# A sigmoid attention and bilinear FFN kernel: weight decoding in six VectorE operations on larger pieces, casts moved to ScalarE, no GpSimd work in the first twelve pairs of heads

## The chip, the core and the metric

The kernel runs on one core of one Trainium2 chip. The metric is the device time of one execution in microseconds (us). Engine names are those of the profile: PE is TensorE (PEld its weight loads), DVE is VectorE, ACT is ScalarE, POOL is GpSimd, SP is SyncE, which here only issues DMAs.

## What is computed

```python
# q, k, v: 8 batches x 12 heads x 448 positions x 64; weights are handed over as float64
scores = q @ k.T / sqrt(64) - log(448)
attn   = 1 / (1 + exp(-scores))            # a sigmoid, no softmax
x      = (attn @ v), heads side by side    # [3584, 768]
h      = (x @ w1) * (x @ w2)               # [3584, 1024]
out    = (h @ w3) @ w_out                  # [3584, 768]
```

## The kernel before

**Precision.** Most products run in float32r passes. An operand x is split into a hi part (a cast to float32r) and a lo part (x minus hi), and a product is hi·hi + hi·lo + lo·hi. So every operand costs a cast and a subtraction somewhere. `split` (L63) is that pair of instructions, with the engine of each given by the caller.

**Weights.** They arrive as float64 words, read as pairs of uint32. `load_words` (L67) brings a piece, `magnitude` (L72) takes the absolute value of the high words on ACT into a tile `f`, and `decode` (L77) makes float32 out of it with seven operations on DVE (L81 to L99; the last, an addition, on POOL for w3). Then `split` makes the hi and lo weights: the cast on DVE, the subtraction on POOL. `decode_weights` (L263) is a generator: one `next` of it (a *take*) issues the loads ahead, the magnitudes ahead, one decode and one split. A piece of w1 or w2 is 128 rows by 384 columns, 32 pieces in all, two for each operand of the product with a chunk of features; w3 follows in 24 pieces that go back to memory.

**Attention and the first product.** The work runs over 48 pairs of heads, six for each batch. A pair has four *slots*, one for each chunk of keys (the short one of 64 keys comes second). Slots are counted from 0, so that pair p begins at slot 4p and batch 1 at slot 24. In a slot PE computes the scores of the chunk (L183), ACT the sigmoid (L168, tile `ap` in plain pairs), and PE multiplies the attention of the slot before by v (L232 in plain pairs, L239 in the others). Two PSUM buffers hold scores. The first twelve pairs are *plain*: attention and v stay in float32 there, and DVE and POOL are left to the weights. From the third slot of batch 1 on (slot 26), PE also computes the product of the batch before with w1 and w2 (L302, tile `up`), twelve matmuls in each slot; a chunk of features takes 36 of them, three slots, and its product `g` (L313) goes to memory.

**Preparation of a pair.** `split_pair` (L136) makes qs, kh and kl of the next pair. It is issued in the second slot of a pair (for pair 1, in the first slot of pair 0). In plain pairs before the change: the cast of q and its lo part on DVE (L141, L142), the cast of k on ACT, kl on POOL; for pairs 0 and 1 all of it on DVE. The loads of q and k share three buffers, so that a load waits until the split two tiles back is done.

**Order.** PE and SP keep to the order in which the code is written, from beginning to end. ACT and POOL do so too for pairs 0 and 1 only (`if p == 2` closes that); after that, and on DVE throughout, a planner orders the instructions. A take that is written in a slot of pairs 0 or 1 thus puts its magnitudes, and any cast of it that is on ACT, ahead of the sigmoid of the next slot.

**Deal of the pieces.** `pieces` says how many takes each slot of batch 0 has (nine in all, the first in slot 3); in batch 1 every slot has one; later batches have four each.

**Afterwards.** While the last batch's product with w1 and w2 runs, w_out is decoded; then w3 w_out (L441) and the final product (L459) follow.

Of the kernel before, what the change touches and what calls it, by code (L numbers as in the profile page):

```python
# [11 lines left out]
F32 = mybir.dt.float32  # L12
# [6 lines left out]
# high words of 2**-127 and 2**128 as float64, read as the float32 of their bits  # L19
HW_MIN, HW_MAX = (float(np.uint32(e << 20).view(np.float32)) for e in (896, 1151))  # L20
# [3 lines left out]
def sigmoid_attention_bilinear_ffn(  # L24
    ctx: ExitStack,
    tc: tile.TileContext,
    qT: bass.AP,     # [B, D, H, S]
    kT: bass.AP,     # [B, D, H, S]
    v: bass.AP,      # [B, S, H*D]
    w1: bass.AP,     # [DM, 2*DF], float64 words as uint32 pairs, as all weights  # L30
    w2: bass.AP,     # [DM, 2*DF]
    w3T: bass.AP,    # [DF (columns of w3), 2*DF (rows of w3)]
    w_out: bass.AP,  # [DF, 2*DM]
    out: bass.AP,    # [B*S, DM]
):
# [100 lines left out]
    def split_pair(plain, first, qq, kk):  # L136
        """q as (hi; lo) in the rows; hi and lo of k, each twice in the rows."""
        qs = pa.tile([P, 2, S], F32R, name="qs")
        kh = pa.tile([P, 2, S], F32R, name="kh")
        kl = pa.tile([P, 2, S], F32R, name="kl")  # L140
        nc.vector.tensor_copy(out=qs, in_=qq)  # L141
        nc.vector.tensor_tensor(out=qs[D:], in0=qq[D:], in1=qs[D:], op=ALU.subtract)  # L142
        if first:
            split(kh, kl, kk, nc.vector.tensor_copy, nc.vector)
        else:
            split(kh, kl, kk, nc.scalar.copy if plain else nc.vector.tensor_copy, nc.gpsimd)
        if plain:
            return qs, kh, kl, None
        # the short chunk of head 0 as (hi, lo), of head 1 as (lo, hi)
        ks = pa.tile([P, 2, P], F32R, name="ks")  # L150
        for j in range(2):
            for i, k in ((j, kh), (1 - j, kl)):
                nc.gpsimd.tensor_copy(out=ks[:, j, i * D:(i + 1) * D], in_=k[:, j, S - D:])
        return qs, kh, kl, ks

    def split_v(plain, vv):
        if plain:
            return vv
        # head 0 as (hi, lo), head 1 as (lo, hi)
        vs = pa.tile([P, NC, 2, 2, D], F32R, name="vs")  # L160
# [9 lines left out]
    def add_halves(dst, src):  # L170
        """Both halves of src[0] to the first half of dst, of src[1] to the second."""
# [14 lines left out]
    def attention(plain, sp):  # L186
        """Attention from its scores, as operands for attend."""
# [12 lines left out]
        al = pa.tile([P, 2, S], F32R, name="al")  # L200
# [3 lines left out]
    def short_scores(ks, qs):  # L204
        """Scores of both heads for the short chunk of keys, head by head in the rows."""
        # kh q and kl q apart, in one pass per head
# [3 lines left out]
        t = pa.tile([P, S], F32, name="st", bufs=1)  # L210
# [3 lines left out]
    def short_attention(t):  # L214
        # hi and lo share the rows of one pass
# [28 lines left out]
    def combine(b, accs):  # L244
# [5 lines left out]
        t = pm.tile([P, S], F32, name="t")  # L250
# [12 lines left out]
    def decode_weights():  # L263
        """w1 and w2 as operands, then w3 as float32 back to memory; a piece at a time."""
        step = NK // 2
        jobs = [
            (n, fc, slice(at, at + step), words(w, slice(fc * P, (fc + 1) * P)))
            for fc in range(NF) for n, w in ((1, w1), (2, w2)) for at in range(0, NK, step)
# [6 lines left out]
        # while attention leaves its buffers of hi and lo idle, they serve here  # L275
        buffers = ((pd, "raw"), (pa, "vs"), (pa, "al"))
        raws, fs = [], []
        for i, (n, at, cs, _) in enumerate(jobs):
            while len(raws) <= min(i + (3 if i < n_up else 1), len(jobs) - 1):
                k = len(raws)  # L280
                _, _, ks, src = jobs[k]
                raws.append(load_words(src[:, ks], *buffers[k // 2 % 3 if k < n_up - 6 else 0]))
            while len(fs) <= min(i + 1, len(jobs) - 1):
# [10 lines left out]
    def up(b, xs, banks):  # L294
        """g = (x w1) * (x w2) of batch b, feature chunk by feature chunk; yields at each matmul."""
# [52 lines left out]
    # a slot per chunk of keys: its scores, products with the first weights, and the slot before's  # L348
    # attention times v; the short chunk of keys second, as it takes longest
    chunks = [0, NC - 1, *range(1, NC - 1)]  # L350
    ups = -(-(NF * 2 * NK * 3) // (NPAIR * NC))
    # pieces of weights per slot of the first batch
    pieces = ((0, 0, 0, 1), (0, 1, 0, 1), (0, 1, 0, 0), (0, 1, 0, 1), (0, 1, 0, 0), (0, 1, 0, 1))
    slot = 0
    for p, (b, hp) in enumerate(pairs):
# [52 lines left out]
    for jc in range(NF):  # L408
        take(filler, 10)
        for half in range(2):  # L410
# [3 lines left out]
            f = decode(raw, magnitude(raw), nc.vector)  # L414
# [77 lines left out]
```

## Time and profile before

| | |
|---|---|
| median of 3 runs | 1121.01 us (1120.77 to 1122.05) |
| span of the profiled execution | 1121.6 us; no time apart from the span is given for it |
| busy: PE, DVE, ACT, POOL | 1084.7, 777.7, 544.4, 295.1 us |
| granted TensorE clock, mean | 0.991 of full |
| DMA traffic | 133.26 MB, 119 GB/s over the span |

The profile is one execution. The busy time of an engine is a sum over the whole span, and the stages of this kernel have different limits: what bounds one of them is read from the idle time of PE in that stage and from what ended it. An instruction whose record is longer than that of others of its kind was held up while it ran.

### The profile page before, as it was taken

To read this page: it belongs to the slowest core of one execution; us is meant where nothing else is said; L and a number is where in the kernel's file an instruction comes from. 1 tells how busy PE (TensorE), PEld (TensorE's weight loads), DVE (VectorE), ACT (ScalarE), POOL (GpSimd) and SP (SyncE) were. 2 spreads that over 40 slices of the span, in tenths; PEclk is the share of its full clock that TensorE was granted. 3 is DMA by queue.
4 is the path that set the end of the run, shared out by engine and by line. 5 is a ranking of instruction groups with operands and counts; after the bars stand their busy time and mean duration, and the time that the engine had idled before them with its cause. 6 is when DMAs were issued, how large, how long until landed. Compare 5 with 4: busy or idle time off the path is not lost.

```text
span 1121.6 us, 15243 instructions
## 1 busy us (share of the span) xinstructions
PE 1084.7 (97%) x5424; PEld 964.5 (86%) x5424; DVE 777.7 (69%) x1281; ACT 544.4 (49%) x780; POOL 295.1 (26%) x322
## 2 busy tenths in 40 slices
PE   6889888999999999999999999999999999999998
PEld 2346656899999999999999998899999999999998
DVE  6999999988888888888888888958932222223222
ACT  4653333677676776767767676673322111111110
POOL 1535435433434344343343434400000000000000
PEclk9889999999999999999999999999999999999999
DMA  9576444553543535435354355305441033333331
GB/s 239 142 196 167 136 110 120 150 136 101 149 109 94 141 101 149 103 97 143 101 149 106 92 145 143 100 27 164 124 130 38 16 123 100 116 114 106 117 106 50
DMA packets 116043, 133.26 MB, mean 119 GB/s; under 512 B 9216, under 2 KB 100608, under 8 KB 115968
## 3 DMA queue, kind: packets, MB, share of 16 engines
q1 hardware_dynamic: 115968, 132.29, 42.5%
q8 instruction: 43, 0.70, 0.3%
q14 instruction: 32, 0.26, 0.1%
HBM read 102.37 MB, written 29.88 MB: 118 GB/s over the span
## 4 chain that ended last, share of the span: by engine, by line
PE 75%; DVE 11%; issue 6%; DMA 4%; POOL 2%; SPq 1%; ACT 1%; DVEq 0%; POOLq 0%; ACTq 0%
PE up L302 31%; PE up L459 21%; PE av L239 8%; PE sp L183 7%; PE up L441 6%; POOL kl L65 1%; DMA raw<-w 1%; DVE raw L96 1%; DVE f L86 1%; PE sp L209 1%; DVE qs L142 1%; DVE f L93 1%; DVE f L99 1%; DVE raw L81 1%; DMA vv<-vL 1%
## 5 line engine op out<-in xcount | busy, mean ns | idle before, releaser
L302 PE MATMUL up<-xh,w 128*128 128x448 f32 x1536 | 467.4, 368 | 2.2 <-ACT a_sb L310 2.2
L302 PEld LDWEIGHTS up<-xh,w 128*128 128x128 f32 x1536 | 289.2, 188 | 29.3 <-ACT a_sb L310 2.6
L302 PE MATMUL up<-xl,w 128*128 128x448 f32 x768 | 281.8, 367 | 0.0
L459 PE MATMUL up<-w,gh 128*128 128x384 f32 x896 | 227.5, 334 | 0.0
L65 POOL TENSOR_TENSOR kl<-kk,kh 128x896 fp32r<-128x896 f32 x46 | 128.7, 2798 | 144.8 <-DVE kh L64 68.2
L459 PEld LDWEIGHTS up<-w,gh 128*128 128x128 f32 x896 | 161.9, 188 | 0.0
L302 PEld LDWEIGHTS up<-xl,w 128*128 128x128 f32 x768 | 144.5, 188 | 13.1
L459 PE MATMUL up<-w,gl 128*128 128x384 f32 x448 | 149.6, 334 | 0.0
L168 ACT ACTIVATE ah<-sp,bias 128x896 fp32r<-128x896 f32 x108 | 108.6, 1006 | 77.3 <-PE sp L183 77.0
L463 DVE COPY o_sb<-up 128x384 f32<-128x384 f32 x56 | 31.2, 558 | 160.2 <-PE up L459 160.2
L201 DVE TENSOR_TENSOR al<-sp,ah 128x896 fp32r<-128x896 f32 x108 | 117.5, 1088 | 23.3 <-ACT sp L168 21.6
L183 PE MATMUL sp<-qs,kh 128*128 128x448 f32 (+1 forms) x312 | 122.0, 391 | 9.1 <-DVE kh L64 8.0
L183 PE MATMUL sp<-qs,kl 128*128 128x448 f32 (+1 forms) x312 | 117.9, 378 | 5.9 <-POOL kl L65 5.5
L64 ACT CAST gh<-graw 128x1024 fp32r<-128x1024 f32 x28 | 29.5, 1053 | 192.0 <-PE up L459 189.3
L65 POOL TENSOR_TENSOR vs<-vv,vs 128x256 fp32r<-128x256 f32 x72 | 58.5, 827 | 188.4 <-DVE vs L64 140.8
L168 ACT ACTIVATE sp<-sp,bias 128x896 f32<-128x896 f32 x108 | 105.1, 973 | 0.0
L183 PEld LDWEIGHTS sp<-qs,kh 128*128 128x128 f32 (+1 forms) x312 | 58.9, 189 | 50.5 <-issue 37.2
L239 PE MATMUL av<-ah,vs 128*128 128x448 f32 x288 | 94.9, 370 | 3.0 <-DVE t L175 2.0
L74 ACT ACTIVATE f<-raw 128x384 f32<-128x384 f32 (+1 forms) x72 | 38.5, 541 | 97.4 <-POOL w L65 39.1
L459 PEld LDWEIGHTS up<-w,gl 128*128 128x128 f32 x448 | 84.1, 188 | 0.0
L239 PE MATMUL av<-al,vs 128*128 128x448 f32 x216 | 80.0, 370 | 4.2 <-DVE al L201 3.9
L65 POOL TENSOR_TENSOR w<-f,w 128x384 fp32r<-128x384 f32 x32 | 48.9, 1532 | 97.0 <-DVE w L64 95.0
(58 smaller groups left out, 1479.6 us busy)
## 6 DMA issues: line engine op xcount, KB each, us to landing
qq<-qT SPq DMA_DIRECT2D x96, 224.0 KB, 3.8
kk<-kT SPq DMA_DIRECT2D x96, 224.0 KB, 3.9
g_dram<-g SPq DMA_DIRECT2D x64, 224.0 KB, 2.0
graw<-g_dram SPq DMA_DIRECT2D x28, 512.0 KB, 3.7
raw<-w SPq DMA_DIRECT2D x32, 384.0 KB, 4.6
out<-o_sb SPq DMA_DIRECT2D x56, 192.0 KB, 1.9
vv<-vL SPq DMA_DIRECT2D x48, 192.0 KB, 3.8
raw<-w3T SPq DMA_DIRECT2D x16, 384.0 KB, 4.1
```

The lines of the kernel that those rows point to most:

```text
L64: hi_engine(out=dst_hi, in_=src)
L65: lo_engine.tensor_tensor(out=dst_lo, in0=src, in1=dst_hi, op=ALU.subtract)
L74: nc.scalar.activation(f, raw[..., 1].bitcast(F32), AF.Abs)
L81: nc.vector.tensor_scalar(out=high, in0=high, scalar1=0x80000000, scalar2=0x40000000, op0=ALU.bitwise_and, op1=ALU.bitwise_xor,)
L168: nc.scalar.activation(dst, src, AF.Sigmoid, bias=bias[:n], scale=scale)
L183: nc.tensor.matmul(sp[:, j], k[:, j, at:at + n], qs[:, j], start=m == 0, stop=m == 1)
L201: nc.vector.tensor_tensor(out=al, in0=sp, in1=ah, op=ALU.subtract)
L239: nc.tensor.matmul(accs[j][:, :S], v[:, c, j].rearrange("p u d -> p (u d)"), a[:, j], start=first and m == 0, stop=last and m == len(ops) - 1,
L302: nc.tensor.matmul(acc[:, :S], w[:, fc, kc], x, start=(kc == 0 and m == 0), stop=(kc == NK - 1 and m == 2),)
L441: nc.tensor.matmul(acc[:, :NM], a[:, jc], w[:, jc, ms], start=(jc == 0 and m == 0), stop=(jc == NF - 1 and m == 2),)
L459: nc.tensor.matmul(acc[:, :NM], a[:, fc], w[:, fc, ms], start=(fc == 0 and m == 0), stop=(fc == NF - 1 and m == 2),)
L463: nc.vector.tensor_copy(out=o_sb[:, ms], in_=acc[:, :NM])
```

## The change

- `decode` has six operations instead of seven. The scale 2^-16 that the magnitude now applies moves the exponent so that a left shift by 3 does what a left shift by 4 and a right shift by 1 did, and shift and exclusive-or become one `scalar_tensor_tensor`. The last addition is on DVE always.
- A piece of w1 or w2 has 768 columns a partition instead of 384: 16 pieces instead of 32, one for each operand and chunk of features. Their raw words have a pool of their own with three buffers (`pp`), closed at pair 11; tiles that only the other pairs need (ks, vs, al, st) then come from a pool `pf` opened in its place. The tile `f` has two buffers instead of three, `t` one instead of two. A piece of w3 has 384 columns as before, or 256.
- The hi cast of a piece of w1 or w2 moves from DVE to ACT, its lo subtraction from POOL to DVE.
- In plain pairs the cast of q moves from DVE to ACT (not for pairs 0 and 1), kl moves from POOL to DVE (it was there for pairs 0 and 1); for pairs 0 and 1 the cast of k moves from DVE to ACT.
- The takes: slots 1, 7, 13 and 19 in batch 0, two slots in three of batch 1 (slots 24, 25, 27, 28, ... 46), later batches as before.

```diff
     def magnitude(raw):
-        f = pd.tile([P, *raw.shape[1:-1]], F32, name="f", bufs=3)
-        nc.scalar.activation(f, raw[..., 1].bitcast(F32), AF.Abs)
+        f = pd.tile([P, *raw.shape[1:-1]], F32, name="f")
+        nc.scalar.activation(f, raw[..., 1].bitcast(F32), AF.Abs, scale=HW_SCALE)
...
         nc.vector.tensor_scalar(out=f, in0=f, scalar1=HW_MIN, scalar2=HW_MAX, op0=ALU.max, op1=ALU.min)
-        nc.vector.tensor_scalar(
-            out=fb, in0=fb, scalar1=4, scalar2=1,
-            op0=ALU.logical_shift_left, op1=ALU.logical_shift_right,
+        nc.vector.scalar_tensor_tensor(
+            out=fb, in0=fb, scalar=3, in1=high, op0=ALU.logical_shift_left, op1=ALU.bitwise_xor
         )
-        nc.vector.tensor_tensor(out=fb, in0=fb, in1=high, op=ALU.bitwise_xor)
...
-        add_engine.tensor_tensor(out=f, in0=f, in1=r, op=ALU.add)
+        nc.vector.tensor_tensor(out=f, in0=f, in1=r, op=ALU.add)
...
-        nc.vector.tensor_copy(out=qs, in_=qq)
+        copy = nc.scalar.copy if plain else nc.vector.tensor_copy
+        (nc.vector.tensor_copy if first else copy)(out=qs, in_=qq)
         nc.vector.tensor_tensor(out=qs[D:], in0=qq[D:], in1=qs[D:], op=ALU.subtract)
-        if first:
-            split(kh, kl, kk, nc.vector.tensor_copy, nc.vector)
-        else:
-            split(kh, kl, kk, nc.scalar.copy if plain else nc.vector.tensor_copy, nc.gpsimd)
+        split(kh, kl, kk, copy, nc.vector if plain else nc.gpsimd)
...
         for i, (n, at, cs, _) in enumerate(jobs):
+            end = n_up if i < n_up else len(jobs)
+            while len(raws) < min(i + (3 if i < n_up else 2), end):
+                _, _, ks, src = jobs[len(raws)]
+                raws.append(load_words(src[:, ks], pp if len(raws) < n_up else pd))
+            while len(fs) < min(i + 2, end):
+                fs.append(magnitude(raws[len(fs)]))
+            f = decode(raws[i], fs[i])
             if n == 3:
-                f = decode(raws[i], fs[i], nc.gpsimd)
                 nc.sync.dma_start(out=w3_dram[at, :, cs], in_=f)
             else:
-                f = decode(raws[i], fs[i], nc.vector)
-                split(wh[n][:, at, cs], wl[n][:, at, cs], f, nc.vector.tensor_copy, nc.gpsimd)
+                split(wh[n][:, at, cs], wl[n][:, at, cs], f, nc.scalar.copy, nc.vector)
...
-    pieces = ((0, 0, 0, 1), (0, 1, 0, 1), (0, 1, 0, 0), (0, 1, 0, 1), (0, 1, 0, 0), (0, 1, 0, 1))
+    pieces = {1, 7, 13, 19} | {NPAIR * NC + i for i in range(3 * NF) if i % 3 < 2}
...
+        if p == PLAIN - 1:
+            take(weights, 2 * NF - len(pieces & set(range(slot))))
+            phase_p.close()
+            pf.append(phase_a.enter_context(tc.tile_pool(name="pf", bufs=2, side="right")))
...
-            if b == 0:
-                take(weights, pieces[hp % len(pieces)][i])
-            elif b == 1 or hp % 3 < 2 and i == 1:
+            if slot in pieces or b > 1 and hp % 3 < 2 and i == 1:
                 take(weights, 1)
```

## Rows read from the trace of the kernel before

**Rows 1.** The page: DVE's busy share in 40 slices of 28 us, in tenths.

```profile
DVE  6999999988888888888888888958932222223222
```

**Rows 2.** Stretches of the span: busy time of each engine, granted clock, DMA share, GB/s.

```profile
core 0: us, PE busy (x) PEld busy (x) DVE busy (x) ACT busy (x) POOL busy (x), PEclk, DMA share, GB/s
10.40:72.80 62.40, 52.77 (x194) 21.90 (x192) 55.28 (x94) 35.84 (x45) 27.22 (x14) 0.89 0.72 183
72.80:185.70 112.90, 104.47 (x471) 72.29 (x469) 109.22 (x209) 44.47 (x66) 48.49 (x33) 0.98 0.56 155
185.70:224.50 38.80, 33.98 (x155) 29.75 (x154) 35.93 (x59) 23.05 (x34) 18.47 (x24) 0.96 0.44 120
224.50:754.40 529.90, 527.52 (x2571) 481.48 (x2570) 437.76 (x689) 375.04 (x543) 200.72 (x247) 1.00 0.44 116
```

**Rows 3.** PE's timeline: start us, us; score matmuls of slots 2, 3, 8, 10, 45, 46.

```profile
15.52 0.47 PE L183 MATMUL sp<-qs,kh 128*128 128x448 f32 x1
...
17.43 0.47 PE L183 MATMUL sp<-qs,kh 128*128 128x448 f32 x1
...
32.09 0.74 PE L183 MATMUL sp<-qs,kl 128*128 128x448 f32 x1 [5.47 <-POOL kl L65]
...
37.95 0.47 PE L183 MATMUL sp<-qs,kh 128*128 128x448 f32 x1
...
172.56 0.47 PE L183 MATMUL sp<-qs,kh 128*128 128x448 f32 x1
...
176.94 0.47 PE L183 MATMUL sp<-qs,kh 128*128 128x448 f32 x1
```

**Rows 4.** Groups of instructions, 0 to 186 us, DVE and POOL: busy, mean ns.

```profile
L99 DVE TENSOR_TENSOR f<-f,raw 128x384 f32<-128x384 f32 x32 | 22.9, 716 | 0.3
L142 DVE TENSOR_TENSOR qs<-qq,qs 64x896 fp32r<-64x896 f32 x14 | 20.7, 1476 | 0.5
...
L95 DVE TENSOR_SCALAR raw<-f 128x384 uint32<-128x384 uint32 x32 | 13.9, 436 | 0.2
...
L65 POOL TENSOR_TENSOR w<-f,w 128x384 fp32r<-128x384 f32 x32 | 48.9, 1532 | 97.0 <-DVE w L64 95.0 <-PE sp L183 2.0
```

**Rows 5.** Timeline of DVE beside POOL: operations alone and beside a GpSimd subtraction.

```profile
7.97 1.09 DVE L65 TENSOR_TENSOR kl<-kk,kh 128x896 fp32r<-128x896 f32 x1
...
9.09 0.63 DVE L141 CAST qs<-qq 128x896 fp32r<-128x896 f32 x1
...
88.33 2.24 POOL L65 TENSOR_TENSOR kl<-kk,kh 128x896 fp32r<-128x896 f32 x1
...
88.50 2.29 DVE L86 TENSOR_SCALAR f<-f 128x384 f32<-128x384 f32 x1
...
92.64 0.35 DVE L86 TENSOR_SCALAR f<-f 128x384 f32<-128x384 f32 x1
...
94.11 0.55 DVE L93 TENSOR_TENSOR f<-f,raw 128x384 uint32<-128x384 uint32 x1
```

**Rows 6.** Timeline, 14 to 24 us, of ACT and DVE: sigmoids, casts, first pieces.

```profile
14.73 1.01 ACT L168 ACTIVATE ap<-sp,bias 128x896 f32<-128x896 f32 x1 [1.59 <-PE sp L183]
...
18.79 0.56 ACT L74 ACTIVATE f<-raw 128x384 f32<-128x384 f32 x1 [1.08 <-DMA raw<-w]
...
19.38 0.36 DVE L81 TENSOR_SCALAR raw<-raw 128x384 uint32<-128x384 uint32 x1 [1.00 <-ACT f L74]
...
19.92 0.55 ACT L74 ACTIVATE f<-raw 128x384 f32<-128x384 f32 x1 [0.57 <-DMA raw<-w]
...
22.58 0.94 ACT L64 CAST kh<-kk 128x896 fp32r<-128x896 f32 x1
...
23.46 0.35 DVE L64 CAST w<-f 128x384 fp32r<-128x384 f32 x1
```

**Rows 7.** Groups of instructions of ACT, whole span: busy, mean ns.

```profile
L74 ACT ACTIVATE f<-raw 128x384 f32<-128x384 f32 x64 | 35.0, 554 | 94.0 <-POOL w L65 39.1 <-DMA raw<-w_out 24.5 <-DMA raw<-w 21.2
L64 ACT CAST woh<-f 128x384 fp32r<-128x384 f32 x16 | 8.0, 511 | 10.2 <-DVE f L99 7.3 <-PE up L302 2.8
```

More of the change, by code (lines that the diff above doesn't have):

```diff
@@ L17 @@
 PSUM = bass.MemoryType.PSUM
-HW_MIN, HW_MAX = (float(np.uint32(e << 20).view(np.float32)) for e in (896, 1151))
+HW_SCALE = 2.0 ** -16
+HW_MIN, HW_MAX = (float(np.uint32((e - 128) << 20).view(np.float32)) for e in (896, 1151))
 @with_exitstack
@@ L65, in split, with load_words @@
         lo_engine.tensor_tensor(out=dst_lo, in0=src, in1=dst_hi, op=ALU.subtract)
-    def load_words(src, pool=pd, tag="raw"):
-        raw = pool.tile([P, *src.shape[1:-1], 2], U32, name="raw", tag=tag, bufs=2)
+    def load_words(src, pool=pd):
+        raw = pool.tile([P, *src.shape[1:-1], 2], U32, name="raw")
         nc.sync.dma_start(out=raw, in_=src)
@@ L72, in magnitude, with decode @@
     def magnitude(raw):
-        f = pd.tile([P, *raw.shape[1:-1]], F32, name="f", bufs=3)
-        nc.scalar.activation(f, raw[..., 1].bitcast(F32), AF.Abs)
+        f = pd.tile([P, *raw.shape[1:-1]], F32, name="f")
+        nc.scalar.activation(f, raw[..., 1].bitcast(F32), AF.Abs, scale=HW_SCALE)
         return f
-    def decode(raw, f, add_engine=nc.gpsimd):
+    def decode(raw, f):
         low, high = raw[..., 0], raw[..., 1]
@@ L81, in decode @@
         nc.vector.tensor_scalar(
-            out=high, in0=high, scalar1=0x80000000, scalar2=0x40000000,
+            out=high, in0=high, scalar1=0x80000000, scalar2=0x80000000,
             op0=ALU.bitwise_and, op1=ALU.bitwise_xor,
@@ L109, in sigmoid_attention_bilinear_ffn @@
     px = (px0, px1)
+    phase_p = ExitStack()
+    pp = phase_p.enter_context(tc.tile_pool(name="pp", bufs=3, side="right"))
     bias = pm.tile([P, 1], F32, name="bias", bufs=1)
@@ L140, in split_pair @@
         kl = pa.tile([P, 2, S], F32R, name="kl")
-        nc.vector.tensor_copy(out=qs, in_=qq)
+        copy = nc.scalar.copy if plain else nc.vector.tensor_copy
+        (nc.vector.tensor_copy if first else copy)(out=qs, in_=qq)
         nc.vector.tensor_tensor(out=qs[D:], in0=qq[D:], in1=qs[D:], op=ALU.subtract)
-        if first:
-            split(kh, kl, kk, nc.vector.tensor_copy, nc.vector)
-        else:
-            split(kh, kl, kk, nc.scalar.copy if plain else nc.vector.tensor_copy, nc.gpsimd)
+        split(kh, kl, kk, copy, nc.vector if plain else nc.gpsimd)
         if plain:
             return qs, kh, kl, None
-        ks = pa.tile([P, 2, P], F32R, name="ks")
+        ks = pf[0].tile([P, 2, P], F32R, name="ks")
         for j in range(2):
@@ L158, in split_v @@
             return vv
-        vs = pa.tile([P, NC, 2, 2, D], F32R, name="vs")
+        vs = pf[0].tile([P, NC, 2, 2, D], F32R, name="vs")
         for j in range(2):
@@ L199, in attention @@
             return (ah,)
-        al = pa.tile([P, 2, S], F32R, name="al")
+        al = pf[0].tile([P, 2, S], F32R, name="al")
         nc.vector.tensor_tensor(out=al, in0=sp, in1=ah, op=ALU.subtract)
@@ L209, in short_scores @@
             nc.tensor.matmul(sp[:, j], ks[:, j], qs[:, j], start=True, stop=True)
-        t = pa.tile([P, S], F32, name="st", bufs=1)
+        t = pf[0].tile([P, S], F32, name="st", bufs=1)
         add_halves(t, [sp[:, j] for j in range(2)])
@@ L249, in combine @@
             return xh, xl
-        t = pm.tile([P, S], F32, name="t")
+        t = pm.tile([P, S], F32, name="t", bufs=1)
         add_halves(t, [acc[:, :S] for acc in accs])
@@ L266, in decode_weights @@
         jobs = [
-            (n, fc, slice(at, at + step), words(w, slice(fc * P, (fc + 1) * P)))
-            for fc in range(NF) for n, w in ((1, w1), (2, w2)) for at in range(0, NK, step)
+            (n, fc, slice(0, NK), words(w, slice(fc * P, (fc + 1) * P)))
+            for fc in range(NF) for n, w in ((1, w1), (2, w2))
         ]
@@ L274, in decode_weights @@
         ]
-        buffers = ((pd, "raw"), (pa, "vs"), (pa, "al"))
         raws, fs = [], []
         for i, (n, at, cs, _) in enumerate(jobs):
[L279 to L283, printed above, removed]
+            end = n_up if i < n_up else len(jobs)
[3 more added lines that the diff above has]
+            while len(fs) < min(i + 2, end):
                 fs.append(magnitude(raws[len(fs)]))
+            f = decode(raws[i], fs[i])
             if n == 3:
-                f = decode(raws[i], fs[i], nc.gpsimd)
                 nc.sync.dma_start(out=w3_dram[at, :, cs], in_=f)
             else:
-                f = decode(raws[i], fs[i], nc.vector)
-                split(wh[n][:, at, cs], wl[n][:, at, cs], f, nc.vector.tensor_copy, nc.gpsimd)
+                split(wh[n][:, at, cs], wl[n][:, at, cs], f, nc.scalar.copy, nc.vector)
             raws[i] = fs[i] = None
@@ L333, in sigmoid_attention_bilinear_ffn @@
     accs = {}
+    pf = []
     def attend_due(slot):
@@ L413, in sigmoid_attention_bilinear_ffn @@
             raw = load_words(src)
-            f = decode(raw, magnitude(raw), nc.vector)
+            f = decode(raw, magnitude(raw))
             split(woh[:, jc, ms], wol[:, jc, ms], f, nc.scalar.copy, nc.vector)
```

## The prediction

> **What bounds the kernel now.** The slices of the page come first: DVE is at 9 tenths in the first seven of forty, 0 to 196 us, and lower after [rows 1]. The stretches say what that does to PE. From 224.5 to 754.4 us PE is busy for 527.5 of 529.9 us at full clock, so nothing done to DVE there can pay. In the two stretches before 185.7 us, which are slots 1 to 24 and slots 25 to 47, DVE is busy 89% and 97% of the time and PE idles 9.6 and 8.4 us; another 4.8 us are idle up to 224.5, and the clock stands at 0.89, 0.98 and 0.96 [rows 2].
>
> What could these stretches be at best? PE's timeline shows two undisturbed paces: 17.43 - 15.52 = 1.91 us for a slot of attention alone, 176.94 - 172.56 = 4.38 us for a slot with twelve `up` matmuls [rows 3]. I call the stretches A, B and C.
> - A, 24 slots of 1.91: 45.8 us. It takes 62.4, an excess of 16.6.
> - B, one of 1.91 and 22 of 4.38: 98.3 us. It takes 112.9, an excess of 14.6.
> - C has 4.8 us of idle PE, and 4% of its 34 busy us as lost clock, 1.4: an excess of 6.2.
>
> Together 37.4 us; 1121.6 - 37.4 = 1084 is the floor for any change to this part. Causes stand in the rows: kl from POOL held PE for 5.47 us until 32.09 [rows 3], and the DVE work is itself stretched. The maximum-minimum takes 0.35 us alone and 2.29 beside a kl subtraction of POOL that starts 0.17 us earlier and lasts 2.24 [rows 5].
>
> **The change, part by part.**
>
> *DVE's decode.* Alone, one-source operations on 384 columns take 0.35 us and two-source ones 0.55 [rows 5]. Two pieces of old size: 2 x (5 x 0.35 + 3 x 0.55) = 6.8 us with the hi cast. The eight groups of this work, of which rows 4 hold the first and the last, sum to 142.5 us for 32 pieces; alone they would be 16 x 6.8 = 108.8. So 33.7 us is stretch. The lo part of q adds 14 x (1.476 - 1.09) = 5.4 [rows 4, 5]. About 39 us of DVE time goes to POOL's company, and the change ends that company in the first twelve pairs.
>
> New durations lie between known sizes. One-source: 0.35 at 384 and 0.63 at 896, so 0.56 at 768. Two-source: 0.55 and 1.09, so 0.95 [rows 5]. A large piece is 3 x 0.56 + 3 x 0.95, and 0.95 more for the lo subtraction: 5.5 us. The fused shift is not in the trace; it is bounded by a one-source and by two chained operations, 0.56 to 1.51, and I take 0.95, the two-source row.
>
> *DVE's sum in B*: 12 pieces x 5.5 = 66; four w3 pieces of 3 x 0.35 + 3 x 0.55 = 2.7 each, 10.8; five plain splits (lo of q and kl, 1.09 each) 10.9 and the one of pair 12, 2.4; six lo parts of x and seven g, both near 0.62, 8.1 (an estimate between the 384 and 896 rows). That makes 98 us against PE's 98.3: no longer late, but without slack. In A it is 4 x 5.5 + 6 x (2.18 + 0.62) = 39 of 45.8 us.
>
> *ACT.* The cast of 896 takes 0.94 us and that of 384 takes 0.511, so that of 768 is 0.83; the magnitude of 384 takes 0.554, of 768 by the same slope 0.88 [rows 6, 7]. In A: 24 sigmoids of 1.01, six times 1.88 for q and k, six casts of x near 0.56, four times 1.71: 45.7 us against PE's 45.8, so ACT is full there and I add 2 us (0 to 8, the 8 being a wait of about 1.9 us behind two casts for four of the pairs). In B it is 23 for sigmoids, 9 for splits, 3 for x, 23 for pieces and 4 for the copies of `up`, 62 of 98: loose.
>
> The Trainium skill ("ScalarE: Activation LUTs", Rules for kernel authors) says that plain arithmetic belongs on VectorE and not on ScalarE. Rows agree on the price of one cast, 0.94 against 0.63 us at 896 columns. By that rule the moved casts would be a loss; by the stage's sums they are one only in A, which the rival "ACT" prices.
>
> *The first take.* In pairs 0 and 1 ACT keeps the written order. The first take moves from slot 3 to slot 1 and now has a cast on ACT, which waits for the whole decode; the sigmoid of slot 2 stands behind it, then at 14.73 us [rows 6]. The first raw piece is now two of the old; the second of the old had landed at 19.92, so the magnitude ends near 20.8. The six operations are 4.5 us alone; the first piece before took 23.46 - 19.38 = 4.1 where its seven are 3.4 - 0.35 = 3.05 alone, as another was interleaved, so 4.5 to 6.1: 25.4 to 26.9. With the cast ACT is free near 27.1, and the sigmoid is 12.4 us late. PE, with two score buffers, can only do slot 3's scores meanwhile. After the 5.5 us wait before, slots 8 and 9 from 32.09 to 37.95 took 5.86 us instead of 3.6 (two slots less a matmul done), at the low clock: 2.3 more [rows 3]. Price 14.7 us, bounds 11 to 19.
>
> Behind the stalled ACT nothing else waits: kh and qs of pair 2 come after. SP issues the three raw loads, 2.36 MB instead of 1.57, ahead of pair 3's q and k; at 183 GB/s [rows 2] the extra 0.79 MB is 4.3 us of transfer within a stall of 12. The second take, in slot 7, has the same order on ACT, but its raw words are there early and DVE is idle during the first stall, so I take nothing (upper bound: decode and cast, 5.4 to 7).
>
> *Other moves.* kh of pair 0 comes from ACT, 0.94 for 0.63: 0.3 us at the start. The wait for `pf` costs nothing while the last large piece (slot 40) is decoded before slot 45; if DVE were four slots late, 17 us, it would hold pair 12. The loads of a third large piece wait for the decode of the one before the current, on SP, with q and k of the next pair behind; these have most of a pair, 17 us, to land. Later w3 pieces gain an addition on DVE and lose a shift: 20 x 0.2 us in a stretch that is PE's, nothing.
>
> *The sum.* A: 45.8 + 14.7 + 2 = 62.5 for 62.4, +0.1. B: 98.3 plus 4 us of excess, a choice between 0 and 11.2 (98 + 12 waits of one sigmoid, 1.01, for the cast to end, less 98.3): 102.3 for 112.9, -10.6. C: DVE arrives without backlog, but pair 12 still brings casts of DVE and subtractions of POOL: 4.5 of 6.2 gone. Start +0.3. 1121.6 + 0.1 - 10.6 - 4.5 + 0.3 = 1106.9 us. The median of the runs shown is 0.6 below that span, so I say 1106.5.
>
> **The rivals.**
> - *DVE stays the bound.* 98 us in B has no slack; each lo subtraction waits about 1 us for ACT, and B reaches 109.5 or more. For: the sum. Against: the idle of DVE behind casts of ACT was small where both work together. B only -3, C -3: 1116, range 1113 to 1120.
> - *ACT becomes the bound in A*, as the skill's rule would have it. Two casts between sigmoids delay scores of two buffers: 6 us on top in A, 1112.
> - *No stall in slot 1*, or most of it hidden: A near 48. Against: the written order. 1121.6 - 14.5 - 10.6 - 4.5 = 1092, and 1098 if half of it remains.
> - *Slower: DVE queues behind ACT's cast at each piece.* Place: the lo subtraction in B. If it stands at DVE's head for s us, B is 98 + 12s. The gain of 14.7 is gone at 102.3 + 14.7 = 117, that is s = 1.6 us. A cast behind a sigmoid, a magnitude and qs and kh would be 3.8 late; at s = 3, B is 134 and the time 1138. For: ACT is a queue and DVE cannot pass. Against: `f` has two buffers, so the next decode can fill the gap if it is ordered there.
> - *No change*: mishaps and gains cancel, 1119 to 1123.
>
> **How the numbers follow.** 0.2% of the time, 2.2 us, is about what a measurement tells from no change. Chances: my forecast (1100 to 1111) 0.42; ACT 0.13; DVE 0.16; no stall 0.13; slower 0.12; no change 0.04. Faster is the sum of the first four, 0.84, less 0.02 for the end of the DVE case: 0.82. Same 0.05, slower 0.13. For 8 in 10 I leave out the slower case and the lower half of the no-stall case: 1094 to 1121. The forecast's own range is 1100 to 1111.
>
> **What would show it.** ACT should idle from about 14 to 26 us for the first hi cast, with a low clock behind it. The first `up` slot should come near 75 us, where it was. DVE operations should keep their lengths alone (0.56 and 0.95) until slot 45. From slot 26 slots should be 4.4 to 4.7 us; pair 12 should begin near 175 us instead of 185.7. The forecast is wrong if DVE's idle ends on the hi cast by more than a microsecond, if the fused shift takes well over 0.95 us, if the ScalarE order lets slot 2's sigmoid pass, or if SP's wait for raw buffers brings q and k late.

## The result and the profile after

The changed kernel takes 1105.97 us (median of 4 runs, 1105.32 to 1108.13), the kernel before 1121.35 (4 runs, 1120.77 to 1122.05): a ratio of 0.986, 95% interval 0.9847 to 0.9873. The prediction was 1106.5 us.

The spans of the two profiled executions, 1121.6 and 1103.5 us, differ by more, 18.1 us. A run's time is 1.8 us above its span (1105.32 and 1103.5 for the profiled one here), so the execution of before that was profiled was one of about 1123.4 us, 2 above the median; the rest is that the one of after was 0.7 below its own.

Line numbers after the change differ by up to four. The page's slices of DVE and POOL, 27.6 us each, answer to [rows 1]:

```profile
DVE  4678997897988879888788987758732122222222
POOL 0000012343433433234333333300000000000000
```

The stretches, cut at the same slots as in [rows 2] (slots 1 to 24, 25 to 48, 49 to 56, then to the end of attention):

```profile
core 0: us, PE busy (x) PEld busy (x) DVE busy (x) ACT busy (x) POOL busy (x), PEclk, DMA share, GB/s
10.46:74.82 64.36, 49.76 (x194) 21.02 (x192) 42.93 (x55) 43.79 (x52) 0.00 (x0) 0.92 0.75 189
74.80:177.00 102.20, 102.20 (x470) 71.40 (x468) 86.44 (x127) 59.15 (x76) 7.63 (x12) 1.00 0.65 179
177.00:208.20 31.20, 31.20 (x155) 28.67 (x154) 29.06 (x50) 21.35 (x32) 10.88 (x14) 1.00 0.59 156
208.20:736.30 528.10, 526.35 (x2570) 481.72 (x2569) 433.41 (x665) 373.78 (x539) 184.95 (x227) 1.00 0.42 112
```

| stretch | before | after | difference | predicted |
|---|---|---|---|---|
| start, to slot 1 | 10.40 | 10.46 | +0.1 | +0.3 |
| A, slots 1 to 24 | 62.4 | 64.4 | +2.0 | +0.1 |
| B, slots 25 to 48 | 112.9 | 102.2 | -10.7 | -10.6 |
| C, slots 49 to 56 | 38.8 | 31.2 | -7.6 | -4.5 |
| slot 57 to the end of attention | 529.9 | 528.1 | -1.8 | 0 |
| w3 w_out and the final product | 367.3 | 367.3 | 0 | 0 |

In B and C PE now never idles and its clock is full. What is left is in A, and the list of PE's waits between 10 and 80 us (engine, what it waited for: us, times, longest) says where:

```profile
PE av L233 <- ACT ap L169: 13.1, 3, 10.4
PE av L233 <- DMA vv<-vL: 1.4, 2, 0.7
```

The longest is the forecast stall of the first take. Its timeline (start us, us; the time idle before in brackets):

```profile
19.68 0.89 ACT L76 ACTIVATE f<-raw 128x768 f32<-128x768 f32 x1 [6.25 <-DMA raw<-w]
20.61 0.56 DVE L83 TENSOR_SCALAR raw<-raw 128x768 uint32<-128x768 uint32 x1 [6.95 <-ACT f L76]
21.94 0.91 ACT L76 ACTIVATE f<-raw 128x768 f32<-128x768 f32 x1 [1.37 <-DMA raw<-w]
...
25.93 0.83 ACT L66 CAST w<-f 128x768 fp32r<-128x768 f32 x1 [3.08 <-DVE f L99]
26.67 1.90 ACT L169 ACTIVATE ap<-sp,bias 128x896 f32<-128x896 f32 x2
27.72 1.76 PE L233 MATMUL av<-ap,vv 128*64 128x448 f32 x4 [10.38 <-ACT ap L169]
```

ACT stood for raw words, then for DVE's last addition, and only then did the two sigmoids that PE needed; they had run from 14.73 on in [rows 6]. Slots 1 to 4, four slots of 1.91 us, took 21.99 us here, 14.35 more than their pace.

The groups of DVE up to 177 us, by shape, answer to [rows 4]; their lengths are those of operations alone:

```profile
L91 DVE SCALAR_TENSOR_TENSOR f<-f,raw 128x768 uint32<-128x768 uint32 x16 | 15.3, 956 | 0.3
L146 DVE TENSOR_TENSOR qs<-qq,qs 64x896 fp32r<-64x896 f32 x14 | 15.3, 1090 | 5.6 <-ACT qs L145 5.2
L67 DVE TENSOR_TENSOR w<-f,w 128x768 fp32r<-128x768 f32 x16 | 15.2, 953 | 2.7 <-ACT w L66 2.6
...
L83 DVE TENSOR_SCALAR raw<-raw 128x768 uint32<-128x768 uint32 x16 | 9.0, 561 | 13.4 <-ACT f L76 13.4
```

### The profile page after: what moved, and what is told of

Same layout as the page of the kernel before. It is cut to its first block, busy times and chain, and to the rows that moved or that the text cites. A ratio compares the mean times of both kernels' runs of the same rounds, so it can differ in the third digit from the quotient of the medians.

```text
span 1103.5 us, 14939 instructions
## 1 busy us (share of the span) xinstructions
PE 1075.5 (97%) x5424; PEld 961.9 (87%) x5424; DVE 729.2 (66%) x1119; ACT 566.2 (51%) x792; POOL 203.7 (18%) x256
## 4 chain that ended last, share of the span: by engine, by line
PE 87%; DVE 5%; DMA 4%; issue 1%; SPq 1%; POOL 1%; ACT 1%; DVEq 0%; ACTq 0%; POOLq 0%
PE up L300 38%; PE up L460 21%; PE sp L184 10%; PE av L240 8%; PE up L442 6%; PE av L233 3%; DMA vv<-vL 2%; PE sp L210 1%; DVE al L202 1%; POOL kl L67 1%; SPq L125 1%; DMA raw<-w 1%; DVE qs L146 0%; DMA g_dram<-g 0%; DMA kk<-kT 0%
## 5 line engine op out<-in xcount | busy, mean ns | idle before, releaser
L67 POOL TENSOR_TENSOR kl<-kk,kh 128x896 fp32r<-128x896 f32 x36 | 102.1, 2836 | 298.2 <-DVE kh L66 234.7
L464 DVE COPY o_sb<-up 128x384 f32<-128x384 f32 x56 | 31.2, 558 | 160.1 <-PE up L460 160.1
L224 DVE TENSOR_TENSOR ah<-st,ah 64x448 fp32r<-64x448 f32 x72 | 49.7, 690 | 26.1 <-ACT st L169 24.5
L184 PEld LDWEIGHTS sp<-qs,kl 128*128 128x128 f32 (+1 forms) x312 | 58.2, 187 | 6.2 <-DVE kl L67 0.8
```

Of the source, the lines that this page charges most:

```text
L67: lo_engine.tensor_tensor(out=dst_lo, in0=src, in1=dst_hi, op=ALU.subtract)
L184: nc.tensor.matmul(sp[:, j], k[:, j, at:at + n], qs[:, j], start=m == 0, stop=m == 1)
L224: nc.vector.tensor_tensor(out=a[others, j], in0=t[rows], in1=a[rows, j], op=ALU.subtract)
L464: nc.vector.tensor_copy(out=o_sb[:, ms], in_=acc[:, :NM])
```

## Experiments

Each kernel was timed in three rounds against the kernel before on the same chip, and all compute everything. The stages are those above, counted from the start of the score matmuls of slots 1, 25, 49 and 57, in one profiled execution of each. The median of the kernel before ranges from 1121.35 to 1123.75 us in this table; differences between rows are uncertain by that much.

| kernel | us | before | ratio (95%) | A | B | C |
|---|---|---|---|---|---|---|
| after | 1105.97 | 1121.35 | 0.986 (0.9847, 0.9873) | 64.4 | 102.2 | 31.2 |
| e5_before_no_pool | 1108.46 | 1121.84 | 0.9876 (0.9853, 0.9898) | 50.2 | 105.7 | 43.5 |
| e4_lo_pool | 1126.58 | 1121.81 | 1.0041 (1.0026, 1.0056) | 72.7 | 113.2 | 34.1 |
| e11_kl_pool | 1118.67 | 1123.75 | 0.9954 (0.9936, 0.9972) | 73.4 | 102.6 | 34.3 |
| e2_first_cast_dve | 1101.26 | 1121.81 | 0.9813 (0.9799, 0.9828) | 62.3 | 102.2 | 31.2 |
| e3_casts_dve | 1105.02 | 1121.81 | 0.9851 (0.9834, 0.9867) | 57.3 | 107.1 | 32.7 |
| e1_late_take | 1100.37 | 1121.81 | 0.9806 (0.9792, 0.9821) | 56.6 | 103.6 | 31.2 |
| e6_early_loads | 1099.31 | 1121.84 | 0.9796 (0.9775, 0.9816) | 55.5 | 103.0 | 31.3 |
| e9_loads_casts | 1099.22 | 1123.75 | 0.979 (0.9765, 0.9815) | 54.7 | 103.0 | 31.5 |
| e10_spread_loads | 1096.01 | 1123.75 | 0.975 (0.9733, 0.9766) | 51.9 | 103.3 | 31.5 |
| e8_small_pieces | 1110.88 | 1121.84 | 0.9896 (0.9877, 0.9914) | 61.5 | 105.3 | 33.3 |
| e7_seven_ops | 1115.65 | 1121.84 | 0.9937 (0.9911, 0.9962) | 66.3 | 102.7 | 37.7 |
| e12_seven_no_w3 | 1112.15 | 1122.78 | 0.9907 (0.9883, 0.9931) | 65.7 | 102.2 | 31.6 |

### GpSimd's company

**The kernel before, with only the subtractions moved** (e5).

```diff
-            split(kh, kl, kk, nc.scalar.copy if plain else nc.vector.tensor_copy, nc.gpsimd)
+            split(kh, kl, kk, nc.scalar.copy if plain else nc.vector.tensor_copy, nc.vector if plain else nc.gpsimd)
...
-                split(wh[n][:, at, cs], wl[n][:, at, cs], f, nc.vector.tensor_copy, nc.gpsimd)
+                split(wh[n][:, at, cs], wl[n][:, at, cs], f, nc.vector.tensor_copy, nc.vector)
```

> The kernel before with one part of the change alone: the lo subtractions of weights and of plain pairs' k go from GpSimd to VectorE. VectorE's work up to 186 us loses 39 us of stretch and gains 32 x 0.55 + 11 x 1.09 = 30, so it ends some 9 us earlier; kl no longer comes late from GpSimd. Theory (the company of GpSimd was the larger part, VectorE stays the bound): 1108 to 1114. Rival (only with fewer and larger operations is anything won): 1119 or more, as the work of VectorE is nearly the same.

13.4 of the 15.4 us come with this alone. Its stretches (A, B, C):

```profile
10.24:60.41 50.17, 46.84 (x193) 19.88 (x191) 44.81 (x97) 35.54 (x45) 0.00 (x0) 1.00 0.91 226
60.41:166.10 105.69, 102.97 (x471) 71.17 (x469) 102.64 (x245) 47.62 (x67) 3.83 (x5) 1.00 0.58 162
166.10:209.56 43.46, 35.30 (x154) 30.69 (x153) 36.46 (x58) 22.44 (x33) 16.46 (x20) 0.92 0.42 112
```

```profile
L99 DVE TENSOR_TENSOR f<-f,raw 128x384 f32<-128x384 f32 x31 | 17.2, 553 | 0.1
L142 DVE TENSOR_TENSOR qs<-qq,qs 64x896 fp32r<-64x896 f32 x13 | 14.2, 1090 | 0.4
```

(DVE groups, 0 to 166 us; [rows 4] have 716 and 1476 ns.) DVE took over some 28 us of subtractions (31 of 0.55, ten of 1.09) and was busy 17 us less in A and B, 147.5 for 164.5: A and B last 155.9 us for 175.3 before. It is 97% busy in B, as before, and C pays (43.5 for 38.8): PE idles there 8.2 us, 5.1 in one wait for DVE's `g` and 2.4 for a piece of weights.

Not all of A's 12.2 us need be DVE's stretch. Of the 9.6 us that PE idled in A of the kernel before, 5.47 were a wait for kl itself [rows 3]: a subtraction of weights, 1.01 us at its shortest, took 5.26 on POOL beside a busy DVE, with kl behind it.

```profile
23.89 5.26 POOL L65 TENSOR_TENSOR w<-f,w 128x384 fp32r<-128x384 f32 x1 [23.45 <-DVE w L64]
29.12 2.92 POOL L65 TENSOR_TENSOR kl<-kk,kh 128x896 fp32r<-128x896 f32 x1
```

e5 ends both, and no run divides the gain between them. Beside e5, the changed kernel shows what the other parts of the change do: they pay in B and C, 3.5 and 12.3 us, and cost 14 in A.

**The changed kernel with its subtractions back on GpSimd** (e4; for weights, and kl from pair 2 on).

```diff
-        split(kh, kl, kk, copy, nc.vector if plain else nc.gpsimd)
+        split(kh, kl, kk, copy, nc.vector if first else nc.gpsimd)
...
-                split(wh[n][:, at, cs], wl[n][:, at, cs], f, nc.scalar.copy, nc.vector)
+                split(wh[n][:, at, cs], wl[n][:, at, cs], f, nc.scalar.copy, nc.gpsimd)
```

> The lo subtractions of weights and, from pair 2 on, kl go back to GpSimd, all else stays. Theory (GpSimd's company stretches VectorE): each such subtraction holds one or two VectorE operations for about its own 2.1 to 2.8 us; VectorE's busy time in slots 25 to 48 goes from 86 to 95 to 105 us, kl comes late, time 1108 to 1118. Rival (fewer and larger operations are what paid): VectorE's slack takes it, time within 2 us of 1106.

It lost more than expected, 20.6 us, and ends 0.4% slower than before. The DVE groups, slots 29 to 48 (98 to 196 us), are stretched:

```profile
L91 DVE SCALAR_TENSOR_TENSOR f<-f,raw 128x768 uint32<-128x768 uint32 x10 | 14.6, 1457 | 0.2
L96 DVE SCALAR_TENSOR_TENSOR raw<-raw 128x768 f32<-128x768 uint32 x10 | 12.6, 1257 | 0.2
L95 DVE TENSOR_SCALAR raw<-f 128x768 uint32<-128x768 uint32 x10 | 11.6, 1162 | 0.1
```

Yet DVE is not full: 86.4 of 98.1 us in that stretch, where PE idles 8.6. A sum of busy time doesn't explain it. PE waits there 4.8 us for ACT's sigmoids and 3.7 for DVE's `g`; ahead of the two longer waits of the first kind ACT stands at a magnitude until POOL's subtraction has freed the tile `f` (2.34 us at 128.01, 1.11 at 140.59), with the sigmoid behind it. The next run shows another chain.

**Only kl of the plain pairs back on GpSimd** (e11; the first of the two edits).

> One part of e4_lo_pool alone: kl of the plain pairs from pair 2 on goes back to GpSimd, the lo subtractions of weights stay on VectorE. Ten kl of 2.2 us each hold one VectorE operation for that long and relieve it of 1.09: net 10 us more on VectorE in the first 177 us, a third of what e4 put there. Theory (VectorE's slack in slots 25 to 48 is 15 us, so that a part fits in): 1106 to 1112. Rival (it is the lateness of kl itself that cost e4 its 20 us): 1115 or more.

The time is the rival's, its reason is not: PE never waits for a kl from POOL in this run. Nor was the place B, which kept its 102.6 us: A lost 9.0 and C 3.1. Slots 13 to 16 took 13.16 us where they took 8.34; the timeline there:

```profile
53.35 0.97 PE L233 MATMUL av<-ap,vv 128*64 128x448 f32 x4 [2.08 <-DMA vv<-vL]
...
54.28 1.09 DVE L146 TENSOR_TENSOR qs<-qq,qs 64x896 fp32r<-64x896 f32 x1
54.41 2.89 POOL L67 TENSOR_TENSOR kl<-kk,kh 128x896 fp32r<-128x896 f32 x1 [6.65 <-ACT kh L66]
55.40 2.72 DVE L99 TENSOR_TENSOR f<-f,raw 128x768 f32<-128x768 f32 x1
...
58.16 0.83 ACT L66 CAST w<-f 128x768 fp32r<-128x768 f32 x1 [3.82 <-DVE f L99]
58.90 1.90 ACT L169 ACTIVATE ap<-sp,bias 128x896 f32<-128x896 f32 x2
...
59.95 0.30 PEld L233 LDWEIGHTS av<-ap,vv 128*64 128x64 f32 x4 [1.11 <-ACT ap L169]
```

POOL's kl, running for 2.1 us where nothing disturbs it, takes 2.89 behind DVE's lo part of q; the last addition of a decode then takes 2.72 for 0.95, ending 0.8 us after kl does. ACT stands 3.82 us at the hi cast that needs it, with two sigmoids behind it, and PE stands behind those. The idle of PE in these 13.16 us is 2.6, and a granted clock of 0.74 takes another 2.7. But of the 2.6 only 0.5 is this chain; 2.08 came before it, for v, whose lateness is not explained. The chain's larger part is in slots 21 to 24, 13.24 us for 8.97:

```profile
74.33 2.09 POOL L67 TENSOR_TENSOR kl<-kk,kh 128x896 fp32r<-128x896 f32 x1 [7.22 <-ACT kh L66]
74.36 2.87 DVE L99 TENSOR_TENSOR f<-f,raw 128x768 f32<-128x768 f32 x1
77.27 0.83 ACT L66 CAST w<-f 128x768 fp32r<-128x768 f32 x1 [3.01 <-DVE f L99]
79.06 1.76 PE L233 MATMUL av<-ap,vv 128*64 128x448 f32 x4 [3.21 <-ACT ap L169]
```

In the kernel after, ACT stood 1.10 us at that cast and PE 1.30 behind it. Over A as a whole PE idled 18.5 us for 14.6 and the clock stood at 0.82 for 0.92, so more than half of the 9.0 us is lost clock; 1.1 of it lies in the first stall, before any kl ran on POOL. A took 72.7 us in e4: what e4 lost in A comes with kl alone, and the 11 us that it lost in B come only once the weights are back on POOL too.

The Trainium skill ("SBUF — State Buffer", Who interferes with whom) says that a DVE instruction with two SBUF inputs contends with a GpSimd instruction that reads SBUF, for a pair of ports that is held exclusively: the 2.89 and the 2.72 agree with turns, DVE, then POOL, then DVE. What [rows 5] show of one operation is here the first link of a chain through a queue that the change itself made (the cast on ACT).

### The first take

**The first hi cast on DVE** (e2).

```diff
-                split(wh[n][:, at, cs], wl[n][:, at, cs], f, nc.scalar.copy, nc.vector)
+                split(wh[n][:, at, cs], wl[n][:, at, cs], f, nc.scalar.copy if i else nc.vector.tensor_copy, nc.vector)
```

> Only the first piece's hi cast goes back to VectorE. If the stall in slot 1 is ScalarE standing at that cast, the sigmoid of slot 2 starts right after the second magnitude, at 22.9 us instead of 26.7, and the time falls by 3.8 us to 1102. If the stall were only the magnitudes' wait for the raw words, nothing changes (1106). If it were all the cast, 10 us go.

The stall shrank as expected: slots 1 to 4 took 17.36 us instead of 21.99, PE's longest wait 6.1 instead of 10.4. Of these 4.6 us A kept 2.1 in the profiled execution, the slowest of the four, as slots 9 to 12 and 21 to 24 took 2.5 us more; the median is 4.7 lower. The magnitudes that wait for raw words remain ahead of the sigmoids.

**The first takes later** (e1).

```diff
-    pieces = {1, 7, 13, 19} | ...
+    pieces = {8, 12, 16, 20} | ...
```

> Theory (the first take's place on ScalarE costs the stall): with the four takes of batch 0 in slots 8, 12, 16 and 20, ScalarE's written order for pairs 0 and 1 holds no magnitude and no cast of weights, so the 10.4 us wait of TensorE at 27.7 us and the low clock behind it go. Slots 1 to 24 take 50 to 53 us instead of 64.4, and the time is 1092 to 1095. Rival (batch 0 is full on ScalarE and by transfers anyway): the same four pieces in fewer slots delay sigmoids elsewhere, slots 1 to 24 stay above 58, time 1099 or more. Rival (weights late): the up product waits for its first pieces at slot 26.

The time missed the forecast by 5 us. The first stall is gone (slots 1 to 4 in 9.50 us), but slots 17 to 20 took 16.00 for 7.61, so only part of it came back. The waits of PE and the stretches from 30 to 60 us say why:

```profile
PE av L233 <- DMA vv<-vL: 3.5, 2, 2.9
PE av L233 <- ACT ap L169: 1.4, 1, 1.4
```

```profile
30.00:40.00 10.00, 10.00 (x44) 4.32 (x42) 3.90 (x4) 7.63 (x10) 0.00 (x0) 1.00 1.08 303
40.00:50.00 10.00, 7.11 (x30) 3.20 (x31) 8.69 (x13) 8.47 (x11) 0.00 (x0) 0.95 0.81 193
50.00:60.00 10.00, 8.56 (x22) 3.31 (x21) 9.87 (x14) 6.00 (x7) 0.00 (x0) 0.54 1.09 240
```

The three raw loads come in one burst at 303 GB/s with all DMA engines busy, and v of the next pair lands 2.9 us late behind it. Then the clock is at 0.54 for ten microseconds.

**The three loads in slot 1, the takes at slots 8, 12, 16, 20** (e6).

```diff
-        raws, fs = [], []
+        raws, fs = [load_words(src, pp) for _, _, _, src in jobs[:3]], []
+        yield
...
-    pieces = {1, 7, 13, 19} | ...
+    pieces = {1, 8, 12, 16, 20} | ...
```

> As e1_late_take, but the loads of the first three raw pieces stay in slot 1, only the takes are in slots 8, 12, 16 and 20. Theory (in e1 the three raw loads at 30 us filled the queues, share 1.08, and brought v of pair 4 late, which cost 2.9 us, the low clock and the slots after): the wait for v goes, slots 1 to 24 take 48 to 52 us instead of 56.6, time 1093 to 1097. Rival (four pieces in 16 slots are too much for VectorE, which was busy 9.87 of 10 us at 50 to 60): slots 17 to 20 stay 5 us or more too long, time 1099 to 1101.

Missed by 2 us and more: the stall moved to slots 9 to 12 (16.85 us). PE's waits and ACT's there:

```profile
30.53 0.97 PE L233 MATMUL av<-ap,vv 128*64 128x448 f32 x4 [3.16 <-DMA vv<-vL]
38.85 1.63 PE L233 MATMUL av<-ap,vv 128*64 128x448 f32 x4 [4.44 <-ACT ap L169]
```

```profile
37.06 0.83 ACT L66 CAST w<-f 128x768 fp32r<-128x768 f32 x1 [4.03 <-DVE f L99]
```

**The same, with the hi casts of the first four pieces on DVE** (e9; `nc.vector.tensor_copy if i < 4 else nc.scalar.copy` in the split of a piece).

> As e6_early_loads, and the hi casts of the four pieces of batch 0 are on VectorE. Theory (in e6 ScalarE stood 4.0 us at the hi cast of the second piece, with the sigmoids of slots 10 and 11 behind it, so TensorE waited 4.4 us and lost its clock): slots 9 to 13 take 11 to 12 us instead of 16.9, time 1092 to 1096. Rival (VectorE at 9.87 of 10 us is the limit there, and gets 2.2 us more): 1098 or more.

ACT's wait at the cast is gone, and nothing clear of the noise was gained, against a forecast of 1092 to 1096: v's 3.56 us late arrival remains, and the clock behind it.

```profile
31.62 1.76 PE L233 MATMUL av<-ap,vv 128*64 128x448 f32 x4 [3.56 <-DMA vv<-vL]
```

**The same, with the three loads one by one** (e10; in slots 1, 3 and 6).

```diff
-        raws, fs = [load_words(src, pp) for _, _, _, src in jobs[:3]], []
-        yield
+        raws, fs = [], []
+        for _, _, _, src in jobs[:3]:
+            raws.append(load_words(src, pp))
+            yield
...
-    pieces = {1, 8, 12, 16, 20} | ...
+    pieces = {1, 3, 6, 8, 12, 16, 20} | ...
```

> As e9_loads_casts, with the three first raw loads issued one each in slots 1, 3 and 6 instead of all in slot 1. Theory (three at once hold back v of pair 2, for which TensorE waited 3.2 us in e6): that wait goes, 2 to 4 us below e9. Rival (the bytes are the same and the queues full up to 30 us, share 1.07): the wait moves to another load, within 1 us of e9.

3.2 us below the kernel beside it, and the fastest version: 1096.01 us, 0.975 of before. The wait for v is 0.43 us; one of 3.30 for ACT is left, behind a magnitude whose raw words are late:

```profile
28.41 0.97 PE L233 MATMUL av<-ap,vv 128*64 128x448 f32 x4 [0.43 <-DMA vv<-vL]
35.58 0.97 PE L233 MATMUL av<-ap,vv 128*64 128x448 f32 x4 [3.30 <-ACT ap L169]
```

```profile
33.73 0.91 ACT L76 ACTIVATE f<-raw 128x768 f32<-128x768 f32 x1 [2.72 <-DMA raw<-w]
```

### Casts, pieces, operations

**All hi casts of w1 and w2 on DVE** (e3; `nc.vector.tensor_copy` in the split of a piece).

> All sixteen hi casts of w1 and w2 go back to VectorE. Theory (slots 25 to 48 are now TensorE's, VectorE has 15 us of slack there): VectorE gains 11 x 0.56 = 6 us in that stretch and it still takes 102 us; ScalarE stands less in slot 1 (3.8 us) and in slot 24 (1.3 us), so 1100 to 1102. Rival (moving the casts off VectorE is what pays): slots 25 to 48 take 106 or more, time 1108 or more.

Neither forecast came true: A gains 7.0 us and B gives 4.9 back, C 1.6; the medians say no change. B's loss is in one place, slots 37 to 40 (22.21 us for 17.45), where a `g` on DVE came behind the decode of two pieces:

```profile
131.71 0.47 PE L300 MATMUL up<-xh,w 128*128 128x448 f32 x1 [2.96 <-DVE g L311]
```

**Pieces of 384 columns, two to a take** (e8).

```diff
-            (n, fc, slice(0, NK), words(w, slice(fc * P, (fc + 1) * P)))
-            for fc in range(NF) for n, w in ((1, w1), (2, w2))
+            (n, fc, slice(at, at + step), words(w, slice(fc * P, (fc + 1) * P)))
+            for fc in range(NF) for n, w in ((1, w1), (2, w2)) for at in range(0, NK, step)
...
-            yield
+            if n == 3 or i % 2:
+                yield
```

(with six raw buffers, four of `f`, and the loads and magnitudes ahead doubled in number.)

> Pieces of 384 columns again, two for each take, six raw buffers and four f of half the size, so that bytes, places and engines are those of the changed kernel. VectorE pays 2 x (3 x 0.35 + 4 x 0.55) = 6.5 us for what takes 5.5, 11 us more in slots 25 to 48: 97 of 102. Theory: hidden there by half, time 1106 to 1112. Rival (the fixed part of an operation does not matter, as neighbours overlap): 1104 to 1107.

4.9 us more, inside the forecast: B 105.3 for 102.2 with DVE 7.4 us busier (93.8), C 33.3. A gained 2.9, 1.8 of it in slots 1 to 4, where the first cast waits for half a piece.

**Seven operations in the decode** (e7).

```diff
-        nc.vector.scalar_tensor_tensor(
-            out=fb, in0=fb, scalar=3, in1=high, op0=ALU.logical_shift_left, op1=ALU.bitwise_xor
+        nc.vector.tensor_scalar(
+            out=fb, in0=fb, scalar1=4, scalar2=1,
+            op0=ALU.logical_shift_left, op1=ALU.logical_shift_right,
         )
+        nc.vector.tensor_tensor(out=fb, in0=fb, in1=high, op=ALU.bitwise_xor)
```

(with the bounds and the scale of before.)

> Seven operations again, on large pieces: 0.56 us more of VectorE for each, 6 us in slots 25 to 48 with 102 - 86 = 16 us of slack. Theory (TensorE is the bound there): that stretch within 2 us, the first stall 0.6 us longer, time 1105 to 1108. Rival (VectorE still sets the pace in places): 1110 or more.

A miss: 9.7 us instead of at most 2, and not in B, which lost 0.5, but 6.5 in C, 1.9 in A and some 1.6 later. SP's queue at the seam, and what SP waited for between 150 and 180 us:

```profile
171.14 0.34 SPq L288 DMA_DIRECT2D w_dram<-f  x1
171.53 0.63 SPq L314 DMA_DIRECT2D g_dram<-g  x1
172.21 1.13 SPq L127 DMA_DIRECT2D qq<-qT  x2
```

```profile
SPq L288 <- DVE f L101: 20.6, 2, 17.2
```

SP stands at the store of a w3 piece until DVE has decoded it, with q and k of pair 13 behind the store. In the kernel after, these loads are issued at 163.85 us; here at 172.21, DVE idles 1.84 us for q until 176.66, and between 175 and 212 us PE waits 2.9 us for a `g` of DVE and 1.2 for vs.

**Seven operations, and no piece of w3 in batch 1** (e12), so that no store stands ahead of pair 13's loads; the 24 takes of w3 fall to the later batches.

```diff
-    pieces = {1, 7, 13, 19} | {NPAIR * NC + i for i in range(3 * NF) if i % 3 < 2}
+    pieces = {1, 7, 13, 19} | {NPAIR * NC + i for i in range(17) if i % 3 < 2}
```

> The kernel after with the old seven-operation decode, and without the four takes of w3 in batch 1, so that no store of a w3 piece stands in SP's queue ahead of the loads of pair 13; the 24 takes of w3 fall to the later batches. Theory (seven operations cost their 6.5 us in pair 12 because the w3 store waits for DVE's decode and holds the q and k of pair 13): slots 49 to 57 fall from 37.7 us to 31 to 33, and the time from 1115.7 to between 1108 and 1111. Rival (DVE's backlog itself makes pair 12 late, whatever SP does): slots 49 to 57 stay at 36 or more and the time at 1114 or more; a version in between, 33 to 36 us, would mean that both have a share.

C fell to 31.6 us, as the theory said, and the loads of pair 13 were issued 14 us earlier:

```profile
157.98 2.29 SPq L127 DMA_DIRECT2D qq<-qT  x2
160.36 1.18 SPq L127 DMA_DIRECT2D kk<-kT  x2
```

The time missed the forecast by 1 us: from slot 57 on the kernel took 3.6 us more than e7, with 3.0 us of small waits of PE for `al` between 210 and 745 us, beside the four w3 pieces that moved there. The edit took 8.4 us of busy time from DVE in B and C (113.8 for 122.1) as well as the store from SP's queue, so how the 6 us of C divide between these two stays open; that the store held the loads is shown, that it did so alone is not.

## Why the prediction was right, and where only its sum was

**DVE's prices held.** The fused shift, which no row had shown, took 0.956 us (0.95 taken); one-source operations 0.56, the others 0.95, kl 1.09, the lo of q 1.09 for 1.476. That the gain comes from ending POOL's work beside DVE is shown by e5 and, from the other side, by e4: e5 alone brings 13.4 of 15.4 us. Two slips carry nothing: the 9s of [rows 1] are slices 2 to 8, 28 to 224 us, not the first seven; and the upper excess of B comes to 11.8 us by its own terms, not 11.2.

**The first stall held**, place and price: 14.35 us for 14.7, the sigmoid 11.9 us late for 12.4 (the casts ended at 26.8 us instead of 27.1). e2 shows how much of it is the cast, 4.6 us; the magnitudes that stand for raw words ahead of the sigmoid account for most of the rest, as the timeline reads. So "no stall in slot 1" fell, and ten microseconds were to be had by dealing the takes and loads otherwise, with the first four casts on DVE (e10).

**A: +2.0 for +0.1.** The term "2 us (0 to 8)" for a full ACT was 4.2: two waits of PE, 1.40 and 1.30 us, behind a magnitude without raw words and behind a hi cast that waited for DVE, and v's loads, 1.4. ACT, forecast at 45.7 us of work in A, has 43.8 of 64.4: it is not short of time, its queue stands. By the Trainium skill's rule ("ScalarE: Activation LUTs", Rules for kernel authors), plain arithmetic on VectorE, the casts would all go back: e3 shows that it holds in A and fails in B, and both by what stands in a queue rather than by the price of a cast; once the loads came early (e9 against e6, 54.7 us for 55.5) it gave next to nothing in A.

**B: right by two errors.** The window of [rows 2] that I called slots 25 to 47 ends at 185.7, where slot 49 begins (its last two rows in [rows 3] are slots 46 and 47, not 45 and 46; the first two are 3 and 4). B is thus one slot of 1.91 and 23 of 4.38 us, 102.6, not 98.3; the excess of before was 10.3, not 14.6. Idle and lost clock in [rows 2] would have told: 8.4 + 2% of 104.5 = 10.5. I then left 4 us of excess that did not occur. With 7.6 for C (below) the floor was 1087, not 1084. That B's forecast met its time is luck.

**DVE had slack where I saw none.** The forecast was 98 us in B; it is busy for 86.4 of 102.2. One large piece was decoded before slot 25 (11 of 12 remain, 5.5 us less). The other part is overlap: the records of DVE in this window sum to 94.5 us, and their union is 86.4. When two pieces are interleaved, the next operation begins before the one ahead of it ends in the records (one of 0.95 us at 92.43, the next at 93.30); durations added up overstate a busy queue by a tenth. So "DVE stays the bound" and the slower rival, DVE behind ACT's cast, fell: DVE idled 2.1 us in all before the lo subtractions of B.

**C: under-sized**, -7.6 for -4.5. C without idle and at full clock is 31.2 us (after, e1 and e2), so its excess before was 7.6; all of it went, not three quarters. It returns in the runs with a backlog on DVE: 37.7 us in e7 (where SP's queue has a share), 43.5 in e5, more than before.

**Span and time.** I put the time 0.6 us below the span, from an execution that was 2 us above the median; a run's time is 1.8 above its own span. The sum was 1106.9 us for a span of 1103.5: 3.4 too long, with 2.4 the other way from the span. This hid most of what A, C and the later slots add up to, and that 1106.5 came within 0.6 us of the median is luck.

## What to carry to other kernels

An in-order queue that holds both a short-deadline step (a sigmoid, the next pair's loads) and a consumer of slow work (a cast behind a decode, a store behind a decode) passes on every delay; look for what stands in front of the deadline before adding up busy time. Check a stage's pace times its slots against idle plus lost clock in the same window: the two must give the same excess. A wait of PE can cost more than its length: in slots 13 to 16 of e11, 2.6 us of idle came with 2.7 of lost clock.

## What the runs showed of the hardware

- An operation of DVE that doesn't need the result of the one ahead begins 0.08 us before that one's record ends (93.30 after 92.43 + 0.95), one that needs it 0.03 us after (21.67 after 21.08 + 0.56, in the first piece); the records of 102 us sum to 94.5, the busy time is 86.4.
- GpSimd's company costs both sides: kl took 2.09 to 2.89 us on POOL, and an addition of 0.95 us on DVE took 2.72 and 2.87 (e11).
- With three raw loads issued at once (303 GB/s in e1), PE waited 2.9 to 3.6 us for a small load, v (e1, e6, e9); with the same three issued in slots 1, 3 and 6, 0.4 us (e10).
- After an idle of PE of 2.9 us in ten the granted clock was 0.54 over the next ten (e1): near the lower of its two levels, 1.2 and 2.4 GHz.
